# A scheduler's table of durations is replaced by measured ones, with a margin on what TensorE reads

## The chip, the cores and the metric

The kernel runs on one core of a Trainium2 chip. The metric is the device time of one launch, in microseconds (us). The core's engines each run their own queue of instructions in order: PE (TensorE, matmuls), DVE (VectorE), ACT (ScalarE), POOL (GpSimd) and SP (SyncE, which issues the DMAs here). An instruction waits at the head of its queue until its inputs are there, and everything behind it waits as well.

## The reference

Three layers in a row, on float32 data. The first is a linear attention with a complex decay per step; the second and third are wide layers on all 3072 tokens.

```python
def _attn_ref(q, k, v, a_re, a_im) -> np.ndarray:
    B, H, S, D = q.shape                       # 4, 8, 768, 48
    mag = np.sqrt(a_re * a_re + a_im * a_im)
    scale = np.minimum(mag, 0.999) / (mag + 1e-06)
    a_re_n, a_im_n = (a_re * scale, a_im * scale)
...
    for t in range(S):
        ar, ai = (a_re_n[:, :, t, :, None], a_im_n[:, :, t, :, None])
        new_re = ar * S_re - ai * S_im
        new_im = ar * S_im + ai * S_re
        kv = np.einsum('bhd,bhe->bhde', k[:, :, t], v[:, :, t])
        S_re, S_im = (new_re + kv, new_im)
        y[:, :, t] = np.einsum('bhd,bhde->bhe', q[:, :, t], S_re)
...
def _moe_ref(x, w_in, w_out) -> np.ndarray:    # 384 -> 2048 -> 384
    h = x @ w_in
    g = np.maximum(h, 0.0) + np.log1p(np.exp(-np.abs(h)))
    return (g @ w_out).astype(np.float32)
...
def _moe2_ref(x, w1, w2, w3, w_out) -> np.ndarray:   # 384 -> 1024 -> 1024 -> 384
    a = x @ w1
    b = x @ w2
    h = a * b @ w3
    return (h @ w_out).astype(np.float32)
```

## The kernel before

**Attention.** The 3072 tokens are 24 chunks of 128 (numbered `u`, six to a sequence). For a chunk, the decays `a` are loaded and normalised into `P` (ACT makes squares, logarithms and exponentials in `nt`; DVE the rest). DVE then runs a scan over pairs of chunks that multiplies the complex decays up: many multiplies into `tm` and additions back into `P`, on ever shorter and then longer strided slices. With the products of the decays DVE scales the queries and keys into `qkp`. PE transposes the keys (`ktp`), and the whole of `qkp` goes out to DRAM (`pd<-qkp`) and comes back in another layout with two gathers (`rs<-pd`). From `rs` PE computes the scores (`sc0`, `sc1`, four heads each), DVE masks them (`am`), and PE makes the chunk's output (`yp`) and the state's update (`stp`). ACT copies the output to `y`, six small DMAs (`y<-y`) move parts of it to other partitions, and it is cast into a block's input, `x` or `xh` with its remainder `xl`. The buffers `rs0` and `rs1` alternate between chunks.

**The wide layers.** Tokens are taken in blocks: block 0 is chunk 0, block 1 is chunks 1 and 2, and blocks 2 to 8 are three chunks (384 columns) each. In the second layer, each of 16 slices of the hidden width is a group of matmuls into `s1`, three ACT steps and a DVE step to `g`, a split of `g` into a rounded part `gh` and a remainder `gl`, and then matmuls that add into three sums `acc`. Blocks 0 and 1 use plain float32 (two records a matmul in the trace), the others three products of rounded parts. The weights arrive as raw float64 bits; DVE converts them (`w32`), interleaved with all this. The third layer runs behind block 8, with `w3` and `w_out` multiplied ahead into one matrix (`wpa`, `bwp`): groups `pa` and `pb`, their product `bg`, its split `bgh` and `bgl`, and again the sums `acc`. DVE meanwhile checks the raw weights (`ckr`) for their range.

**What sets the order.** The program records every instruction first (`Plan.add`), each with a cost on its engine and a latency until others may use its result, both from a fixed table in `cost`. `wait` gives the delay between a producer and a consumer. `together` makes one piece of a chunk's `yp` and `stp` matmuls. `flush` then runs a list scheduler (`run`): whenever an engine is free in the plan, it takes the most urgent instruction that is ready in the plan. It does so 16 times, each with priorities from the one before, and the plan that ends first is written out. The chip sees the resulting order of each queue and nothing of the planned times. DMAs are issued by SP in that order too.

So the table never costs time itself. Every record has the line of the recorded call (L185 before), so rows are told apart by the names of tiles.

Of the kernel before, what the change touches and what calls it, by code (L numbers as in the profile page):

```python
# [71 lines left out]
class Plan:  # L72
# [49 lines left out]
    def cost(self, eng, op, outs, ins):  # L122
        n = max(self.free_size(x) for x in (*outs, *ins))
        if eng == "SP":
            size = 4
            for _, n in outs[0].ap:
                size *= n
            cost = max(650 if n < 512 and self.on_chip(ins[0]) else 475, size / 360)
            return cost, 1100 + size / 360 + (950 if self.on_chip(outs[0]) else 2300) - cost
        if eng == "PE":  # L130
            n = self.free_size(outs[0])
            if op == "transpose":
                return 109, 200
            m = outs[0].ap[0][1]
            if ins[0].dtype == F32R:
                return max(n / 2.4 + 3, m / 1.2), 200
            return (0.73 * n + 38 if m <= 64 else max(n, m) / 0.6 + 5), 200
        if eng == "DVE":
            return 69 + n / (1.92 if op == "tensor_scalar" else 0.96), 200
        if eng == "ACT":  # L140
            return 120 + n / 1.4, 200
        return 160 + n * 2.08, 200

    def push(self, eng, call, pre, cost, lat):
        self.ops.append((eng, call, pre, cost, lat))
        return len(self.ops) - 1

    def add(self, engine, op, args, kw):
# [35 lines left out]
        def call():  # L184
            getattr(engine.unit, op)(*args, **kw)  # L185

        cost, lat = self.cost(engine.name, op, outs, ins)
        if self.group is None:
            me = self.push(engine.name, [call], pre, cost, lat)
# [17 lines left out]
    @contextmanager  # L207
    def together(self):

        self.group = self.push(None, [], set(), 57, 0)  # L210
        yield
        self.group = None

    def wait(self, p, s):
        eng, _, _, _, lat = self.ops[p]
        if eng == self.ops[s][0]:
            return {"DVE": 127, "PE": 0, "SP": lat}.get(eng, 200)
        return lat

    def run(self, before, after, ready, key, free):  # L220
# [1021 lines left out]
```

## Time and profile before

| | us |
|---|---|
| median of 3 runs | 995.36 |
| lowest and highest run | 994.29, 999.29 |
| the profiled execution's own time | 992.5 |
| its span, first to last instruction | 990.8 |
| PE busy | 885.4 |
| DVE busy | 786.6 |
| ACT busy | 530.6 |

The profiled execution is one run, taken with the hardware profiler; its rows give each instruction's start and duration, and a gap in front of an instruction is put down to what arrived last. Busy PE and DVE overlap almost wholly, so what counts is where PE stands idle, and whether DVE has room at that place.

### The profile page before, as it was taken

How to read it: one execution, taken by the hardware profiler on the slowest of the kernel's cores; microseconds unless marked ns; L12 is line 12 of the kernel's file. 1: busy time of each engine (PE TensorE's matmuls, PEld its weight loads, DVE VectorE, ACT ScalarE, POOL GpSimd, SP SyncE). 2: the span in 40 equal slices, each digit the busy share in tenths (PEclk: the TensorE clock that was granted, in tenths of full speed). 3: DMA queues.
4: the chain of work that ended last, by engine and by line, in shares of the span. 5: the costliest groups of instructions: out<-in, count | busy, mean ns of one | idle time of the engine just before them, and what ended most of it. 6: DMA issues, size and time to landing. Idle time of an engine off the chain costs nothing.

```text
span 990.8 us, 16846 instructions
## 1 busy us (share of the span) xinstructions
PE 885.4 (89%) x6169; PEld 859.6 (87%) x6169; DVE 786.6 (79%) x1773; ACT 530.6 (54%) x1132; POOL 5.4 (1%) x13
## 2 busy tenths in 40 slices
PE   0026999899999999999999989999999999999996
PEld 0026888798899999999999989999999999999996
DVE  6999999999999999999897587999888876322222
ACT  4246685677678686877876576564222222223222
POOL 2000000000000000000000000000000000000000
PEclk9999999999999999999999999999999999999998
DMA  8763744355454654455463465466888774010000
GB/s 307 243 188 80 174 117 121 109 119 120 118 156 115 157 127 122 115 111 162 118 147 105 104 170 166 137 174 201 240 263 265 223 240 157 1 48 25 1 25 27
DMA packets 84618, 138.67 MB, mean 140 GB/s; under 512 B 8112, under 2 KB 56880, under 8 KB 84528
## 3 DMA queue, kind: packets, MB, share of 16 engines
q1 hardware_dynamic: 84528, 137.53, 50.0%
q8 instruction: 50, 0.82, 0.4%
q14 instruction: 40, 0.33, 0.1%
HBM read 108.00 MB, written 28.31 MB: 138 GB/s over the span
## 4 chain that ended last, share of the span: by engine, by line
PE 48%; DVE 32%; DMA 12%; ACT 4%; issue 3%; SPq 0%; DVEq 0%; ACTq 0%
PE acc L185 17%; PE pa L185 8%; PE s L185 8%; PE pb L185 8%; DVE tm L185 7%; DVE P L185 7%; DMA rs<-pd 4%; PE wpa L185 3%; DVE qkp L185 2%; DVE g L185 2%; DVE w L185 2%; PE sc L185 2%; DMA a<-a_in 2%; DVE gl L185 2%; DMA ckr<-w3t 2%
## 5 line engine op out<-in xcount | busy, mean ns | idle before, releaser
L185 DVE TENSOR_TENSOR tm<-P 128x90 f32<-128x90 f32 (+3 forms) x240 | 145.4, 614 | 1.0
L185 ACT ACTIVATE e<-e 128x384 f32<-128x384 f32 (+2 forms) x288 | 136.5, 487 | 3.3
L185 DVE TENSOR_TENSOR bg<-pa,be 128x384 f32<-128x384 f32 x64 | 35.1, 554 | 90.4 <-PE pa L185 54.7
L185 ACT ACTIVATE e<-s 128x384 f32<-128x384 f32 (+2 forms) x144 | 64.4, 450 | 52.5 <-PE s L185 46.5
L185 DVE TENSOR_TENSOR P<-tm 128x45 f32<-128x45 f32 (+11 forms) x304 | 85.1, 341 | 1.2
L185 DVE SCALAR_TENSOR_TENSOR g<-s,e 128x384 f32<-128x384 f32 (+2 forms) x144 | 73.5, 513 | 11.6 <-ACT e L185 11.5
L185 PE MATMUL ktp<-ident,qkp 128*128 128x128 f32 x120 | 21.8, 288 | 67.3 <-DVE qkp L185 66.7
L185 ACT COPY be<-pb 128x384 f32<-128x384 f32 x64 | 30.4, 479 | 91.0 <-PE pb L185 88.7
L185 PEld LDWEIGHTS ktp<-ident,qkp 128*128 128x128 f32 x120 | 16.1, 149 | 69.4 <-issue 59.6
L185 ACT CAST bgh<-bg 128x384 fp32r<-128x384 f32 x64 | 32.7, 514 | 80.0 <-DVE bg L185 79.8
L185 PE MATMUL sc<-rs 112*128 112x128 f32 x384 | 58.3, 289 | 18.1 <-DMA rs<-pd 16.0
L185 PEld LDWEIGHTS sc<-rs 112*128 112x128 f32 x384 | 54.3, 202 | 21.0 <-issue 7.4
L185 DVE TENSOR_TENSOR gl<-g,gh 128x384 fp32r<-128x384 f32 x112 | 62.1, 557 | 10.0 <-ACT gh L185 9.7
L185 ACT CAST gh<-g 128x384 fp32r<-128x384 f32 x112 | 56.6, 508 | 20.9 <-DVE g L185 20.3
L185 DVE CUSTOM_DVE_ANT_0 ck<-ckr 128x384 f32<-128x384 f32 x80 | 43.4, 543 | 20.4 <-DMA ckr<-w3t 7.2
L185 DVE TENSOR_TENSOR bgl<-bg,bgh 128x384 fp32r<-128x384 f32 x64 | 35.1, 554 | 16.8 <-ACT bgh L185 16.3
L185 DVE TENSOR_REDUCE lims<-ck 128x1 f32<-128x384 f32 x80 | 43.0, 537 | 2.0
L185 PE MATMUL acc<-g,w 128*128 128x128 f32 (+1 forms) x192 | 39.9, 337 | 4.7 <-DVE g L185 4.7
L185 PE MATMUL wpa<-wo,w 128*128 128x384 f32 x192 | 41.8, 336 | 0.0
L185 ACT ACTIVATE nt<-a 128x768 f32<-128x768 f32 x24 | 20.3, 844 | 37.3 <-DMA a<-a_in 28.1
L185 PE MATMUL s<-x,w 128*128 128x128 f32 (+1 forms) x192 | 38.9, 338 | 1.2 <-ACT y L185 1.2
L185 DVE TENSOR_TENSOR am<-sc,mask 128x512 f32<-128x512 f32 x48 | 33.0, 688 | 8.4 <-PE sc L185 8.2
(323 smaller groups left out, 2569.7 us busy)
## 6 DMA issues: line engine op xcount, KB each, us to landing
pd<-qkp SPq DMA_DIRECT2D x24, 768.0 KB, 4.4
rs<-pd SPq DMA_DIRECT2D x48, 384.0 KB, 5.8
wr<-wio SPq DMA_DIRECT2D x32, 384.0 KB, 6.4
ckr<-wio SPq DMA_DIRECT2D x32, 384.0 KB, 3.6
a<-a_in SPq DMA_DIRECT2D x24, 384.0 KB, 3.4
qk<-qk_in SPq DMA_DIRECT2D x24, 384.0 KB, 3.3
w3r<-w3t SPq DMA_DIRECT2D x16, 384.0 KB, 3.9
w12r<-w SPq DMA_DIRECT2D x16, 384.0 KB, 3.6
```

The lines of the kernel that those rows point to most:

```text
L185: getattr(engine.unit, op)(*args, **kw)
```

## The change

The durations in `cost` are replaced. A DMA's latency no longer follows one formula: writes to DRAM count 5.2 us to landing, transfers inside the chip 2.3, loads from a DRAM tile of the kernel's own (that is `rs<-pd` and the reload of a block's `x`) 6.8, loads of inputs 2.5 plus size. Matmuls in rounded float32 go from n/2.4 + 3 to n/2.4 + 14 ns, short float32 ones get shorter, DVE operations with two widely strided inputs almost twice as long, ACT operations 105 + 0.88 n in place of 120 + n/1.4. A `together` group starts at 150 ns in place of 57. And `wait` adds 500 ns wherever PE is the consumer, 1500 if the producer is a DMA.

```diff
             cost = max(650 if n < 512 and self.on_chip(ins[0]) else 475, size / 360)
-            return cost, 1100 + size / 360 + (950 if self.on_chip(outs[0]) else 2300) - cost
+            if not self.on_chip(outs[0]):
+                land = 5200
+            elif self.on_chip(ins[0]):
+                land = 2300
+            elif hasattr(ins[0].tensor, "tag_meta"):
+                land = 6800
+            else:
+                land = 2500 + size / 360
+            return cost, max(land - cost, 0)
...
             if ins[0].dtype == F32R:
-                return max(n / 2.4 + 3, m / 1.2), 200
+                return n / 2.4 + 14, 250
...
         if eng == "DVE":
-            return 69 + n / (1.92 if op == "tensor_scalar" else 0.96), 200
+            far = [x for x in ins if x.ap[-1][0] >= 4 and x.ap[-1][1] > 1]
+            return 72 + n / (1.92 if op == "tensor_scalar" else 0.52 if len(far) > 1 else 0.95), 200
...
     def wait(self, p, s):
...
+        if self.ops[s][0] == "PE":
+            return lat + (1500 if eng == "SP" else 500)
         return lat
```

All queues keep the same instructions. Three places show how they move.

First, PE around the first scores of chunk 8 (`sc8_0`, which reads the gathered `rs0`), from the last transposes of the chunk's keys (`ktp8`). Before:

```order
L185 MATMUL ktp8_0_571<-ident_106,qkp8_529 128x128 x3
L185 MATMUL acc_472<-gh_2_9_551,ww8h_533 128x384
L185 MATMUL acc_470<-gl_2_8_539,ww8h_533 128x384
L185 MATMUL acc_470<-gh_2_9_551,ww8h_533 128x384
L185 MATMUL sc8_0_584<-rs0_121 128x128 x4
```

In the changed kernel, the last rows ahead of the same scores (47 matmuls of 384 columns now stand behind the last transpose):

```order
L194 MATMUL acc_472<-gl_2_10_561,ww10h_555 128x384
L194 MATMUL acc_471<-gl_2_10_561,ww10h_555 128x384
L194 MATMUL acc_470<-gh_2_11_569,ww10h_555 128x384
L194 MATMUL acc_470<-gh_2_11_569,ww11l_565 128x384
L194 MATMUL acc_471<-gh_2_11_569,ww10h_555 128x384
L194 MATMUL acc_471<-gh_2_11_569,ww11l_565 128x384
L194 MATMUL sc8_0_584<-rs0_121 128x128 x4
L194 MATMUL sc8_1_595<-rs0_121 128x128 x4
```

The scores moved behind the sums of slices 9, 10 and part of 11 of block 2, and both halves now stand together.

Second, PE between chunk 2's state update (`stp2`) and block 1, whose input is chunk 1's and chunk 2's output. Before, the rows that follow it:

```order
L185 MATMUL stp2_305<-v2_227,kT_123 48x48
L185 MATMUL s1_0_14_309<-x0_190,w32_14_293 128x128 x3
L185 MATMUL acc_216<-g_0_12_296,w32_12_278 128x128
L185 MATMUL acc_214<-g_0_12_296,w32_12_278 128x128
L185 MATMUL acc_216<-g_0_13_303,w32_13_287 128x128
L185 MATMUL acc_214<-g_0_13_303,w32_13_287 128x128
L185 MATMUL s1_0_15_312<-x0_190,w32_15_300 128x128 x3
L185 MATMUL acc_215<-g_0_12_296,w32_12_278 128x128
L185 MATMUL acc_215<-g_0_13_303,w32_13_287 128x128
L185 MATMUL sc3_0_333<-rs1_122 128x128 x3
```

In the changed kernel:

```order
L194 MATMUL stp2_305<-v2_227,kT_123 48x48
L194 MATMUL sc3_0_333<-rs1_122 128x128 x4
L194 MATMUL sc3_1_345<-rs1_122 128x128 x4
L194 MATMUL yp3_351<-rs1_122,S2_307 48x128 x2
L194 MATMUL yp3_351<-am3_0_334,v3_291 48x128 x2
```

The rest of block 0 now stands ahead of chunk 2's output. Between that and block 1 only chunk 3's scores, output and state update are left, with its `yp` directly behind its scores.

Third, DVE ahead of the second half of chunk 1's `qkp`, whose write lets its DMA start. Before:

```order
L185 TENSOR_SCALAR w32_9_255<-wr9_237 128x768
L185 TENSOR_TENSOR P1_141<-tm_165 128x96 x2
L185 TENSOR_SCALAR w32_10_262<-wr10_247 128x768
L185 TENSOR_TENSOR tm_166<-P1_141 128x192
L185 TENSOR_TENSOR n21_172<-n21_172,qk1_168 128x384
L185 TENSOR_TENSOR P1_141<-tm_166 128x48 x2
L185 SCALAR_TENSOR_TENSOR w32_9_255<-wr9_237,w32_9_255 128x768
L185 TENSOR_TENSOR tm_167<-P1_141 128x90
L185 TENSOR_TENSOR qkp1_179<-P0_133,n21_172 128x6x128
L185 TENSOR_TENSOR tm_167<-P1_141 128x90
L185 TENSOR_TENSOR qkp1_179<-P0_133,qk1_168 128x6x128
```

In the changed kernel:

```order
L194 SCALAR_TENSOR_TENSOR w32_9_255<-wr9_237,w32_9_255 128x768
L194 TENSOR_TENSOR tm_165<-P1_141 128x384
L194 TENSOR_TENSOR n21_172<-n21_172,qk1_168 128x384
L194 TENSOR_TENSOR P1_141<-tm_165 128x96 x2
L194 TENSOR_TENSOR qkp1_179<-P0_133,qk1_168 128x6x128
L194 TENSOR_TENSOR tm_166<-P1_141 128x192
L194 TENSOR_TENSOR qkp1_179<-P0_133,n21_172 128x6x128
L194 TENSOR_TENSOR P1_141<-tm_166 128x48 x2
L194 SCALAR_TENSOR_TENSOR w32_8_248<-wr8_229,w32_8_248 128x768
L194 TENSOR_TENSOR tm_167<-P1_141 128x90
```

Steps of the scan (`tm`, `P1`) and of the conversions (`w32_8`, `w32_10`) that stood ahead of `qkp1` stand behind it now.

## Rows read from the trace of the kernel before

**Rows 1.** The page: busy us, share and instructions; shares of the chain that ended last.

```profile
PE 885.4 (89%) x6169; PEld 859.6 (87%) x6169; DVE 786.6 (79%) x1773; ACT 530.6 (54%) x1132; POOL 5.4 (1%) x13
...
PE 48%; DVE 32%; DMA 12%; ACT 4%; issue 3%; SPq 0%; DVEq 0%; ACTq 0%
```

**Rows 2.** Busy time of each engine by stretch: from:to length, then busy (instructions).

```profile
core 0: us, PE busy (x) PEld busy (x) DVE busy (x) ACT busy (x) POOL busy (x), PEclk, DMA share, GB/s
0.00:59.70 59.70, 0.02 (x1) 0.05 (x1) 51.87 (x107) 18.64 (x32) 5.42 (x13) 1.00 0.74 258
59.70:87.70 28.00, 15.20 (x156) 13.72 (x156) 25.81 (x61) 13.61 (x24) 0.00 (x0) 0.94 0.66 155
87.70:257.20 169.50, 154.33 (x1215) 142.04 (x1214) 164.57 (x374) 119.60 (x285) 0.00 (x0) 0.99 0.49 123
257.20:393.30 136.10, 132.69 (x1044) 128.82 (x1043) 131.62 (x297) 102.38 (x220) 0.00 (x0) 1.00 0.52 130
393.30:594.30 201.00, 196.25 (x1545) 191.65 (x1544) 170.52 (x368) 143.89 (x309) 0.00 (x0) 1.00 0.52 130
594.30:983.90 389.60, 386.94 (x2217) 383.31 (x2215) 241.93 (x573) 132.44 (x267) 0.00 (x0) 1.00 0.46 139
```

**Rows 3.** PE's waits from 87.7 to 257.2: total us, times, longest.

```profile
PE sc L185 <- DMA rs<-pd: 4.9, 3, 2.2
PE acc L185 <- DVE g L185: 4.7, 5, 2.2
PE yp L185 <- DVE am L185: 1.3, 1, 1.3
PE s L185 <- ACT y L185: 1.2, 2, 0.8
PE sc L185 <- DVE am L185: 1.0, 1, 1.0
```

**Rows 4.** PE's waits from 257.2 to 594.3.

```profile
PE sc L185 <- DMA rs<-pd: 6.5, 3, 2.6
PE sc L185 <- DVE am L185: 1.1, 1, 1.1
PE acc L185 <- ACT gh L185: 0.3, 1, 0.3
```

**Rows 5.** DMA issues of the page, and the landings of `rs`, issued by SP.

```profile
rs<-pd SPq DMA_DIRECT2D x48, 384.0 KB, 5.8
...
DMA to landing us min/median/max: 4.3/5.8/7.8
```

**Rows 6.** PE's timeline at chunk 8: start, us, operation [idle before <-releaser].

```profile
238.47 1.13 PE L185 MATMUL sc<-rs 112*128 112x128 f32 x8 [2.19 <-DMA rs<-pd]
```

**Rows 7.** The chain that ended last: start, us, operation and count, near the end.

```profile
975.32 7.47 PE acc L185 x43
```

**Rows 8.** DVE groups by shape: count, busy us, mean ns of one, idle before.

```profile
L185 DVE TENSOR_TENSOR am<-sc,mask 128x512 f32<-128x512 f32 x48 | 33.0, 688 | 8.4 <-PE sc L185 8.2
...
L185 DVE TENSOR_TENSOR tm<-P 128x768 f32<-128x768 f32 x12 | 18.6, 1553 | 0.1
```

**Rows 9.** Timeline from chunk 5's output to block 2's first matmul.

```profile
176.88 0.39 PE L185 MATMUL yp<-am,v 128*48 128x128 f32 x4
...
178.03 1.17 ACT L185 COPY y<-yp 48x512 f32<-48x512 f32 x2
...
178.62 3.67 SPq L185 DMA_DIRECT2D y<-y  x6
...
185.38 0.87 PE L185 MATMUL s<-xh,ww0h 128*128 128x384 f32 x3
```

**Rows 10.** PE's timeline at chunk 1's scores.

```profile
80.77 3.59 PE L185 MATMUL sc<-rs 112*128 112x128 f32 x16 [3.96 <-DMA rs<-pd]
```

**Rows 11.** DVE's waits from 87.7 to 257.2.

```profile
DVE am L185 <- PE sc L185: 2.6, 3, 1.4
```

More of the change, by code (lines that the diff above doesn't have):

```diff
@@ L132, in cost @@
             if op == "transpose":
-                return 109, 200
+                return 109, 250
             m = outs[0].ap[0][1]
             if ins[0].dtype == F32R:
-                return max(n / 2.4 + 3, m / 1.2), 200
-            return (0.73 * n + 38 if m <= 64 else max(n, m) / 0.6 + 5), 200
+                return n / 2.4 + 14, 250
+            return (0.75 * n + 24 if m <= 64 else max(n, m) / 0.6 + 5), 250
         if eng == "DVE":
-            return 69 + n / (1.92 if op == "tensor_scalar" else 0.96), 200
+            far = [x for x in ins if x.ap[-1][0] >= 4 and x.ap[-1][1] > 1]
+            return 72 + n / (1.92 if op == "tensor_scalar" else 0.52 if len(far) > 1 else 0.95), 200
         if eng == "ACT":
-            return 120 + n / 1.4, 200
+            return 105 + 0.88 * n, 200
         return 160 + n * 2.08, 200
@@ L208, in together @@
     def together(self):
-        self.group = self.push(None, [], set(), 57, 0)
+        self.group = self.push(None, [], set(), 150, 0)
         yield
```

## The prediction

> **What bounds the kernel now.** I read the busy table of the page first [rows 1]: TensorE is busy 885.4 us of a span of 990.8, VectorE 786.6. Both averages hide stages, so next come the stretches, cut where a block's first matmul runs: 87.7 us is the first matmul of block 0, 257.2 that of block 3, 393.3 that of block 5, 594.3 that of block 8 [rows 2]. Up to 59.7 us TensorE has nothing and VectorE works alone. From 87.7 to 257.2 TensorE is busy 154.33 of 169.5 us and VectorE 164.57: VectorE has 4.9 us of idle time there, so it is the closer bound. From 257.2 to 393.3 it is 132.69 and 131.62 of 136.1. From 393.3 to 594.3 TensorE leads, 196.25 against 170.52 of 201.0, and from 594.3 to 983.9 it runs at 386.94 of 389.6 with VectorE half idle. So what can still be won is TensorE's idle time: 15.2 us from 87.7 to 257.2, 3.4 to 393.3, 4.8 to 594.3, 2.7 to 983.9, and the first of these only as far as VectorE allows.
>
> Then the waits: who held TensorE up. From 87.7 to 257.2 the five largest make 13.1 us: scores waiting for the gathered rows `rs` 4.9, output sums waiting for `g` 4.7, and 3.5 for others [rows 3]. From 257.2 to 594.3 they are 6.5 for `rs`, 1.1 for `am`, 0.3 for `gh` [rows 4]. The reader is to see that 11.4 of these are six waits of up to 2.6 us for one kind of DMA: TensorE stands in order, so everything behind a score waits with it.
>
> **The change, part by part.** No instruction is added or removed; only places in the queues change, so every term is a wait that goes or comes.
>
> *DMA landings.* The old table lets `rs` land 3.1 us after its issue (1100 + 1092 + 950 ns), the new one 6.8, and 1.5 more before TensorE may use it. The trace has a median of 5.8 us, and 4.3 to 7.8 between the ends [rows 5]. So the old plan put scores about 3 us ahead of their data, and the new one puts them a little behind. Chunk 8 shows it: three 384-column matmuls stood between its last transpose and its first score, and TensorE waited 2.19 us [rows 6]; now 47 stand there. At 173.7 ns each (43 in 7.47 us, [rows 7]) the 44 more are 7.7 us. The other five waits are covered too, by my count of the rows: chunk 4 gets 23 matmuls where none stood, chunk 7 gets 73 for 1, chunk 9 some 13.6 us of block 3 for 2.4, chunk 17 gets 19 matmuls more (3.3 us), chunk 23 gets 15 more (2.6 us, as long as its wait, the longest; and its `qkp` has fewer VectorE rows ahead).
>
> Here a page of the Trainium skill speaks against the change. "DMA: Bandwidth & Descriptors", section "Anatomy of one DMA — SWDGE (gpsimd) path", fits about 2.0 us plus bytes over 436 GB/s; for 393,216 bytes that is an estimate of 2.9 us, and by it the old 3.1 was right and all six waits would have another cause. The trace's shortest landing is 4.3 us, on a hardware queue and from a scattered read, so the measurement decides.
>
> *Engine durations.* The old table gives a 384-column matmul 163 ns, the new one 174; the trace 173.7. It gives a strided 768-element multiply on VectorE 869 ns, the new one 1549; the trace 1553 with the tail that overlaps the next instruction, and 12 of them stand in the scans [rows 8]. Its old plan thus let both engines drift late against their partners by different amounts.
>
> "TensorE: Matmul & The Clock Gate" in the Trainium skill, section "Back-to-back issue gap", has N/2.4 + 2.5 ns for matmuls by themselves, an estimate of 162.5 ns for 384 columns. By that the old figure was the right one; the 173.7 of this trace decides for the new one.
>
> *The margin.* Every input of TensorE now counts as 500 ns after its producer's latency. In order, TensorE runs what stands first, so a margin costs nothing while other rows fill it. Counted over the rows, the work between a block's `s1` group and the first sum that reads its `g` grows in every block (smallest gap in block 0 from 2.3 to 3.7 us). That covers the 4.7 us of waits for `g`.
>
> *What comes in its place.* A TensorE that waits less runs out of rows sooner. A block can't begin before the last chunk's output has been copied, shifted by six small DMAs and cast. In chunk 5 that took from 177.3 us (176.88 + 0.39) to 185.4: 8.1 us with little to spare [rows 9]. In the old order the work between that output and the next block was more than this, or about it: 10.2, 7.5 and 9.8 us ahead of blocks 1, 2 and 3, counted in rows. In the new one it is some 6, 5.5 and 7. The rows show it for block 1: sums and `s1` groups of block 0 stood between, now only chunk 3's own work. I expect new waits of about 2, 2.5 and 1 us, 5.5 together, and 1.5 at chunk 3, where the `yp` group stands right behind its scores and has to wait for both `am`, 0.69 us each.
>
> *The head.* The scores of chunk 1 waited 3.96 us for `rs` [rows 10]. Of VectorE's rows ahead of `qkp1`, a step each of `w32_8` and `w32_10` and three short steps of the scan have gone behind it, some 2 us by my count, while chunk 0's `am` moves back by as much. I take 1 us, between 0 and 2.
>
> **The sum**, against the profiled execution's own 992.5 us:
> - head: −1 (0 to −2).
> - 87.7 to 257.2: 13.1 us of listed waits go, 5.5 + 1.5 come, which leaves 6; VectorE gives at most its 4.9 us of idle time, of which 2.6 are waits for scores [rows 11]. I take −4, most of it (0 to −9.8, which is TensorE's 15.2 less the 5.5).
> - 257.2 to 594.3: idle 8.2, of which 7.9 listed; one new wait of 1 at block 5. I take −6 (0 to −8.2).
> - 594.3 to the end: −0.5 of 2.7. The order of the check rows alters little there.
>
> Together −11.5: 981.0. The median of the runs shown lies 2.9 us above the profiled execution and the lowest run 1.8, so I add 2: **983**.
>
> **The rivals.**
> - *More is won.* VectorE turns out not to be the limit, because its idle time and its late starts both shrink with the better durations: all the lower bounds, −2 −9.8 −8.2 −2.7 = −22.7, give 972. For it: TensorE's margins grow nearly everywhere in the new order. Against: VectorE at 97% from 87.7 to 257.2. Chance 0.17, taking in what lies below 978.
> - *The waits only move.* The waits for `rs` and `g` reappear as waits at the block starts and for `am`. If VectorE sets the pace up to 393.3, the first part and the 3.4 us after it are worth nothing, and of the 4.8 after that some 2 stay: 992.5 + 2 − 1 − 2 = about 992. For it: VectorE has 32% of the chain that ended last [rows 1], though TensorE alone sets the pace behind 594.3. Chance 0.18.
> - *Slower: scores too late for VectorE.* VectorE runs in order too, and its `am` stands where it stood, while chunk 8's scores move back by 7.7 us of TensorE's rows. If TensorE hasn't won that much by then, VectorE stands at `am` with the scan queued behind it, in the stretch in which it has only 4.9 us to give. With nothing won the 7.7 come on top: 992.5 + 2 + 7.7 − 2 = about 1000. It decides once TensorE's gain ahead of chunk 8 is below some 4 us. The page on DMAs would make this the likely case, its landings being too short for such a late place; the 4.3 to 7.8 us in the trace make it the unlikely one. Chance 0.10.
>
> **Chances and range.** My forecast, 978 to 990, has 0.55. About 0.5%, 5 us, is what a measurement of this kernel can tell from no change. So faster than 990.4: 0.55 + 0.17 = 0.72; within: 0.18; slower: 0.10. The range of 8 in 10 goes from 971 (just under the case in which all is won) to 996 (half-way from the moved waits to the slower case).
>
> **What would show it.** Waits of scores for `rs` behind 100 us: from 11.4 us to under 3. Waits of sums for `g`: under 2. TensorE's waits for `y` or `xh` at block starts: a new row of 3 to 7 us. The first matmul of block 3 at about 252 in place of 257.2, that of block 8 at about 583 in place of 594.3, and the time behind block 8 unchanged within 2 us. VectorE's waits for scores shouldn't exceed 8 us from 87 to 257. I'm wrong if block 3 begins later than 257, or if the gain is lost again between 393 and 594, where VectorE has room.

## The result, and the profile after

The changed kernel takes 980.34 us in the median of 4 runs (979.71 to 981.5), the kernel before 994.83 (994.19 to 999.29, 4 runs). The ratio is 0.9847, with a 95% interval of 0.982 to 0.9874: faster by 1.5%. The forecast was 983, with 971 to 996. The profiled execution of the changed kernel is one of 979.78 us; its span is 978.0, 12.8 less than before.

The stretches come first again, now cut where the same matmuls run: block 0's first at 88.0 us, block 3's at 250.6, block 5's at 385.1, block 8's at 582.3 (columns as in [rows 2]). The last cut alone is not the same one: 983.9 in [rows 2] lies behind the closing matmul `okt`, 970.0 here lies ahead of it.

```profile
core 0: us, PE busy (x) PEld busy (x) DVE busy (x) ACT busy (x) POOL busy (x), PEclk, DMA share, GB/s
0.00:57.50 57.50, 0.00 (x0) 0.01 (x1) 51.06 (x106) 18.39 (x32) 5.42 (x13) 1.00 0.75 265
57.50:88.00 30.50, 17.00 (x157) 15.27 (x157) 29.18 (x68) 15.27 (x27) 0.00 (x0) 0.89 0.63 148
88.00:250.60 162.60, 153.39 (x1227) 141.97 (x1227) 160.95 (x367) 118.27 (x284) 0.00 (x0) 1.00 0.49 121
250.60:385.10 134.50, 133.28 (x1055) 129.98 (x1055) 130.14 (x294) 104.70 (x224) 0.00 (x0) 1.00 0.57 144
385.10:582.30 197.20, 195.94 (x1533) 191.29 (x1534) 174.20 (x375) 140.82 (x304) 0.00 (x0) 1.00 0.51 131
582.30:970.00 387.70, 383.63 (x2201) 380.75 (x2199) 241.09 (x566) 131.66 (x265) 0.00 (x0) 1.00 0.45 138
```

Against [rows 2]: block 0 starts 0.3 us later, the stretch from block 0 to block 3 is 6.9 us shorter (169.5 to 162.6), and that from block 3 to block 8 is 5.4 shorter (337.1 to 331.7). From block 8 to the end of the last sum (982.78 us before, 969.87 now) it is 0.9 shorter (388.5 to 387.6), and what follows is as long as before (8.0 and 8.1). From block 3 to block 8 PE now stands idle 2.5 us (331.7 − 133.28 − 195.94), where it was 8.2. DVE's idle time from block 0 to block 3 fell from 4.9 to 1.7 us (162.60 − 160.95). DVE also has 3.6 us less to do there (164.57 to 160.95). For 2.6 of it, six more of its instructions now run ahead of block 0: 80.24 us of work (51.06 + 29.18) in place of 77.68 (51.87 + 25.81). The other 1.1 moved behind the beginning of block 3.

PE's waits from block 0 to block 3 (88.0 to 250.6 us) answer to [rows 3]: total us, times, longest.

```profile
PE s L194 <- ACT xh L194: 3.5, 2, 1.9
PE s L194 <- ACT x L194: 2.2, 2, 1.5
PE ktp L194 <- DVE g L194: 1.5, 3, 0.8
PE yp L194 <- DVE am L194: 1.2, 1, 1.2
PE s L194 <- DVE g L194: 0.6, 1, 0.6
PE sc L194 <- DMA rs<-pd: 0.4, 1, 0.4
```

Those from there to block 8 (582.3 us) answer to [rows 4]:

```profile
PE s L194 <- ACT xh L194: 2.5, 2, 1.6
PE sc L194 <- DVE g L194: 0.8, 1, 0.8
PE sc L194 <- DVE am L194: 0.4, 1, 0.4
PE stp L194 <- DVE g L194: 0.2, 1, 0.2
```

The wait of 1.6 us for `xh` is that of block 3's first matmul; it stands at the cut and is in both lists. The scores' 11.4 us for the gathered rows have become 0.4, and the sums' 4.7 for `g` are gone from the list. In their place stand `s` groups that wait for `x` and `xh`: PE has used up its block and waits for the next one's input. The transfers themselves are no faster. Their landings in the changed kernel:

```profile
DMA to landing us min/median/max: 4.3/6.1/8.1
```

In the head, PE's timeline shows why nothing came of the 1 us. The first line is from the kernel before, the rest from the changed one:

```profile
74.84 1.08 PE L185 MATMUL yp<-am,v 128*48 128x128 f32 x16 [0.83 <-ACT nt L185]
...
68.39 3.75 PE L194 MATMUL sc<-rs 112*128 112x128 f32 x16 [0.95 <-DMA rs<-pd]
75.31 1.89 PE L194 MATMUL yp<-am,v 128*48 128x128 f32 x16 [3.17 <-issue]
76.92 1.89 PE L194 MATMUL stp<-v,kT 128*64 128x48 f32 x32
78.87 1.13 PE L194 MATMUL sc<-rs 112*128 112x128 f32 x8
81.73 1.64 PE L194 MATMUL sc<-rs 112*128 112x128 f32 x8 [1.73 <-ACT y L194]
...
88.00 3.65 PE L194 MATMUL s<-x,w 128*128 128x128 f32 x30 [0.69 <-ACT x L194]
```

The scores of chunk 1 no longer wait for the gathered rows (3.96 us in [rows 10]), but chunk 0's `yp` now waits 3.17 us, and the second half of chunk 1's scores 1.73. The first is put down to no producer by the profile, but DVE's second `am` of chunk 0 ends at 75.21 us, 0.1 us ahead of `yp`. It ended at 74.73 before, although chunk 0's scores now begin 1.9 us sooner (68.39 against 70.31).

The clock takes part in this as well. Busy time by stretch, the first line again from the kernel before:

```profile
80.70:84.40 3.70, 3.63 (x18) 3.54 (x20) 1.80 (x5) 0.84 (x1) 0.00 (x0) 0.55 0.25 81
...
75.30:78.90 3.60, 3.53 (x49) 3.40 (x49) 3.60 (x9) 1.56 (x2) 0.00 (x0) 0.53 0.95 169
81.70:86.20 4.50, 4.47 (x40) 4.21 (x42) 4.50 (x9) 4.03 (x8) 0.00 (x0) 0.62 0.07 15
```

A granted clock of 0.53 is 1.2 GHz, the lower of its two levels, for nearly the whole stretch. Before, one such stretch followed the wait of 3.96 us; now one follows the wait of 3.17 and one that of 1.73. The 16 matmuls of `yp` took 1.89 us where they took 1.08. In sum PE starts 2.2 us sooner (57.5 against 59.7), is busy 1.8 us longer in the head (15.20 to 17.00, mean clock 0.94 to 0.89) and idle 0.7 longer (12.80 to 13.50), which makes the 0.3.

### The profile page after: what moved, and what is told of

Its sections match the earlier page's. It is cut to its first block, busy times and chain, and to the rows that moved or that the text cites. A ratio compares the mean times of both kernels' runs of the same rounds, so it can differ in the third digit from the quotient of the medians.

```text
span 978.0 us, 16869 instructions
## 1 busy us (share of the span) xinstructions
PE 883.5 (90%) x6169; PEld 859.3 (88%) x6169; DVE 787.4 (81%) x1773; ACT 529.5 (54%) x1132; POOL 5.4 (1%) x13
## 4 chain that ended last, share of the span: by engine, by line
PE 64%; DVE 10%; DMA 7%; issue 2%; ACT 1%; SPq 0%; DVEq 0%; ACTq 0%
PE acc L194 23%; PE s L194 14%; PE pa L194 8%; PE pb L194 8%; PE sc L194 3%; PE yp L194 3%; PE wpa L194 3%; DMA a<-a_in 2%; DVE tm L194 2%; DMA ckr<-wio 2%; DVE P L194 2%; DMA ckr<-w 1%; PE stp L194 1%; DVE ck L194 1%; DVE g L194 1%
## 5 line engine op out<-in xcount | busy, mean ns | idle before, releaser
L194 PEld LDWEIGHTS ktp<-ident,qkp 128*128 128x128 f32 x120 | 15.6, 148 | 68.6 <-issue 57.5
L194 PE MATMUL sc<-rs 112*128 112x128 f32 x384 | 53.0, 285 | 4.3 <-ACT y L194 1.7
L194 PEld LDWEIGHTS sc<-rs 112*128 112x128 f32 x384 | 50.3, 198 | 6.2 <-ACT y L194 1.9
L194 PE MATMUL yp<-am,v 128*48 128x128 f32 x384 | 36.9, 282 | 4.4 <-issue 3.2
L194 ACT COPY xob<-acc 128x384 f32<-128x384 f32 x24 | 11.4, 481 | 52.5 <-PE acc L194 37.4
L194 PE MATMUL wpa<-wo,w 128*128 128x384 f32 x192 | 39.1, 334 | 0.0
L194 PE MATMUL s<-x,w 128*128 128x128 f32 (+1 forms) x192 | 36.0, 330 | 3.1 <-ACT x L194 2.2
```

## The experiments

The change has three parts: the landings of the DMAs, the durations of the engines, and the margin in `wait`. Each kernel below computes everything. Times are medians with the ratio to runs of the kernel before on the same chip, and its 95% interval. The waits named are those of scores for the gathered rows from 100 to 600 us, unless another stretch is given; the kernel before has 11.4 us of them in six waits.

**Each part alone, and the two without the margin.** The edits take the change's own lines, one part at a time:

```diff
 # d_only: the landings alone
+            if not self.on_chip(outs[0]):
+                land = 5200
...
 # e_only: the costs of PE, DVE and ACT, and of a group, alone
+                return n / 2.4 + 14, 250
...
 # m_only: the margin alone
+        if self.ops[s][0] == "PE":
+            return lat + (1500 if eng == "SP" else 500)
 # de: the changed kernel without the margin
```

> The kernel before with the new DMA landings alone. My theory (each part of the table removes its own waits): the scores' waits for the gathered rows fall from 11.4 us behind 100 us to under 3, sums still wait 3 to 5 us for g, and the time is some 6 us shorter, about 988 to 990. If the margin does it all: no change, 995. If any other order is simply as good as any other and the one before was an unlucky one: a time anywhere from 980 to 1000 that doesn't follow the waits for the gathered rows.

Measured: 984.84 us, ratio 0.9892 (0.987 to 0.9914). No wait for the gathered rows is left; sums wait 2.1 us for `g` from 100 to 250 us, less than the 3 to 5 I had expected. The landings alone give some 70% of the gain (1.1 of 1.5%), more than I had expected.

> The kernel before with the new durations of PE, DVE and ACT alone. My theory: the waits for the gathered rows stay near 11 us, since the landings are as before; the drift of PE and DVE against each other shrinks, so waits of sums for g fall below 3 us; about 990. If the landings do it all: 995. If the order is luck: anything from 980 to 1000.

Measured: 1035.11 us, ratio 1.0389 (1.0361 to 1.0417). This is far outside what any of the theories gave: the measured durations by themselves cost 38 us (1035.11 against 997.06 before on the same chip), the "40 us" of what follows. PE's waits from 100 to 600 us begin with

```profile
PE sc L186 <- DMA rs<-pd: 27.4, 12, 4.3
PE ktp L186 <- DVE qkp L186: 1.6, 1, 1.6
```

and DVE, whose `am` stands in its queue for the scores, waits from 60 to 700 us (8.2 us in the kernel before):

```profile
DVE am L186 <- PE sc L186: 32.9, 25, 4.1
```

So my theory, that each part removes its own waits, falls. Sums wait only 0.5 us for `g` from 100 to 250 us, but twelve waits for the gathered rows came, and both engines stood still in them. The granted clock fell too. Busy time in five stretches of 20 us of this kernel:

```profile
220.00:240.00 20.00, 17.34 (x115) 16.85 (x115) 15.70 (x28) 12.26 (x26) 0.00 (x0) 0.91 0.30 85
240.00:260.00 20.00, 16.64 (x138) 15.55 (x134) 17.52 (x34) 12.32 (x28) 0.00 (x0) 0.91 0.42 92
...
340.00:360.00 20.00, 15.69 (x90) 15.37 (x89) 15.21 (x28) 13.48 (x30) 0.00 (x0) 0.91 0.70 169
360.00:380.00 20.00, 17.87 (x144) 17.20 (x143) 16.63 (x49) 11.25 (x24) 0.00 (x0) 1.00 0.49 112
380.00:400.00 20.00, 20.00 (x167) 19.67 (x166) 20.00 (x39) 17.36 (x36) 0.00 (x0) 1.00 0.44 119
```

A mean of 0.91 is a part of the stretch at 1.2 GHz and the rest at 2.4; it stands where PE had idle time, though not in every such stretch. Over the span PE is busy 904.9 us with the same 6169 matmul records that took 885.4 before [rows 1]. These 19.5 us are somewhat under half of the 44.8 by which the profiled span is longer (1035.6 against 990.8). The lower clock is my reading of them, and its size fits: the mean granted clock of the span is 0.974 against 0.994, so 26.9 us of full clock were not granted (0.026 × 1035.6) against 5.9, 21 us more. Of the other 25.3 us, all idle time, 20.7 are waits for the gathered rows: over the whole span they rose from 16.0 to 36.7.

> The kernel before with the margin alone: 500 ns on what PE reads, 1500 on what it reads from a DMA. My theory: 3.1 + 1.5 us still falls short of a median landing of 5.8, so 4 to 8 us of waits for the gathered rows stay; waits for g and am nearly go; about 988 to 990. If the margin does it all: 980. If the measured durations do it all: 995.

Measured: 990.25 us, ratio 0.994 (0.9915 to 0.9965); 4.5 us of waits for the gathered rows in five waits. The time and these waits came as expected. What I had wrong is `g`: its waits did not nearly go. Sums still wait 2.3 us for it in one wait (3.4 before), and `sc`, `s` and `ktp` groups 6.1 us more.

> The changed kernel without the margin: landings and engine durations as measured. My theory: waits for the gathered rows under 4 us (6.8 covers most landings, 1.5 of margin is missing), waits for g of 2 to 4 us, about 983 to 986. If the margin does it all: 995. If the margin only delays PE: faster than with it, 976.

Measured: 985.85 us, ratio 0.9897 (0.9875 to 0.9919); no wait for the gathered rows, and one block starts with a wait of 5.1 us for `xh`. Within the expectation; beside the landings alone the durations add nothing that these intervals can tell.

**Which number the 40 us hang on.** A new theory: in an exact plan of PE no slack is left by accident, so a false landing costs in full. The first kernel below adds to the engine durations only the 6.8 us for loads from the kernel's own DRAM tiles; the second changes one number of the kernel before.

```diff
 # e_rs: e_only, and
-            return cost, 1100 + size / 360 + (950 if self.on_chip(outs[0]) else 2300) - cost
+            land = 6800 - cost if not self.on_chip(ins[0]) and hasattr(ins[0].tensor, "tag_meta") else 0
+            return cost, max(land, 1100 + size / 360 + (950 if self.on_chip(outs[0]) else 2300) - cost)
 # b_pe174: the kernel before, and
-                return max(n / 2.4 + 3, m / 1.2), 200
+                return n / 2.4 + 14, 200
```

> The engine durations, and of the landings only the 6.8 us for loads from the kernel's own DRAM tiles (the gathered rows and a block's reload). Theory A: the 1035 us with the engine durations alone come from the gathered rows' old 3.1 us, which an exact plan of PE no longer covers by accident; then this one number takes back nearly all of it, 984 to 990, with under 4 us of waits for the gathered rows and a granted clock above 0.99. Theory B: the engine durations themselves give a bad order (DVE's strided cost or ACT's put rows in the wrong places); then it stays above 1010.

Measured: 987.69 us, ratio 0.9904 (0.9879 to 0.9928), granted clock 0.995. From 100 to 600 us no wait for the gathered rows is left; PE's largest group of waits there is

```profile
PE s L187 <- ACT xh L187: 2.9, 1, 2.9
```

One number takes back 47 us from 1035.11. Theory A holds and B falls, for the set of durations as a whole.

> The kernel before with one number changed: a matmul in rounded float32 costs n/2.4 + 14 ns, not n/2.4 + 3. Theory A: the old 163 ns let the real PE run late against its plan, which hid DMA landings; with 174 the waits for the gathered rows rise above 18 us and the time to 1005 to 1030. Theory B: one correct number does no harm, 990 to 997.

Measured: 1021.18 us, ratio 1.0233 (1.0203 to 1.0262). The time is where theory A put it, but its reason is only partly there. PE's largest groups of waits from 100 to 600 us:

```profile
PE sc L185 <- DMA rs<-pd: 12.1, 7, 2.8
PE acc L185 <- ACT gh L185: 5.8, 6, 1.7
PE s L185 <- ACT xh L185: 4.2, 4, 2.4
PE acc L185 <- DVE g L185: 2.3, 4, 0.9
```

Those for the gathered rows rose only from 11.4 to 12.1 us, not above 18. What rose is the others: for `gh` from 0.8 (0.3 of it in [rows 4]) to 5.8, for `xh` from nothing to 4.2. Behind 600 us another 7.2 in eight waits are for `bgh` (0.2 before), and 4.0 in the head are for `x`. Over the whole span PE waits 23.3 us for ACT's `x`, `xh`, `gh` and `bgh`, where it was 1.0. The profiled span is 28.8 us longer (1019.6): 17.2 of it idle time, 11.6 busy time (897.0), at a mean granted clock of 0.988. It seems that the short price of a matmul had hidden ACT's steps: the old table prices one of 384 columns at 394 ns, the new one at 443, and with all engine durations replaced these waits for ACT are only 4.0 us. No run changed ACT's price by itself, so this stays a reading. That one true number alone does harm is shown for this seed; no second one was run for it.

**Is it the draw?** The scheduler has one noisy round, so another seed gives another order with the same table.

```diff
-SEED = 214
+SEED = 1
```

> The kernel before with another seed of the scheduler's one noisy round. If the table decides: within 1% of before, 987 to 1003, with 8 to 20 us of waits for the gathered rows. If the order of before is an unlucky or a lucky draw: more than 1% off.

Measured: 997.62 us, ratio 1.0014 (0.9997 to 1.003); 14.5 us of waits for the gathered rows in eleven. Against this one other seed, the kernel before was no unlucky draw.

> The changed kernel with the same other seed. If the table decides: 975 to 988, again with under 4 us of waits for the gathered rows. If its gain is a draw: 990 or more.

Measured: 987.87 us, ratio 0.99 (0.9871 to 0.9928); no wait for the gathered rows from 100 to 600 us, one of 4.9 in the head. Still 1% faster than before, but 0.5% slower than with seed 214.

> The engine durations alone with seed 1. Theory A: again far slower than before, 1015 to 1045, with over 15 us of waits for the gathered rows. If the 1035 us were a bad draw of the scheduler: 1005 or less.

Measured: 1018.19 us, ratio 1.0239 (1.0202 to 1.0277); 19.6 us of waits in eleven. The engine durations alone are slow with this seed too, by 22 us (996.01 before on this chip) in place of 38. With this table the two seeds are 17 us apart.

> The changed kernel without the margin, with seed 1, beside 985.9 with seed 214 and 987.9 for the margin with seed 1. If the margin is worth something beyond the draw: 990 to 996. If it is only a draw: 980 to 989.

Measured: 987.88 us, ratio 0.9927 (0.9901 to 0.9953), beside 987.87 with the margin and the same seed. With seed 1 the margin is worth nothing. And beside the engine durations alone with the same seed, the true landings take back 30 us (1018.19 to 987.88).

**The margin without the landings, and a shorter landing.** The first kernel is the changed one with the old line for DMAs, the second has one number changed:

```diff
 # em: the old landings
+            return cost, 1100 + size / 360 + (950 if self.on_chip(outs[0]) else 2300) - cost
 # a_rs29
-                land = 6800
+                land = 2900
```

> The changed kernel with the old DMA landings: engine durations and margin, so the gathered rows count as 3.1 + 1.5 us. Theory A (an exact PE plan needs slack ahead of every PE input, and either a true landing or a margin gives it): the margin takes back most of the 40 us of the engine durations alone, 988 to 1000; waits for the gathered rows 4 to 12 us, since 4.6 us is still short of most landings. Theory C (only the true landing of the gathered rows matters): it stays above 1015.

Measured: 992.98 us, ratio 0.9965 (0.9948 to 0.9983), with 4.4 us of waits for the gathered rows in four. The margin takes back 42 us from 1035.11, so theory C falls: slack ahead of every input does nearly what the true landing does.

> The changed kernel with 2.9 us in place of 6.8 for loads from the kernel's own DRAM tiles, the estimate from the Trainium skill's page on DMA; the margin of 1.5 us stays. My theory: 4.4 us is below the median landing of 5.8, so 5 to 10 us of waits for the gathered rows come back, and the time is 985 to 995. If the landing of the gathered rows doesn't matter beside the margin: 978 to 983.

Measured: 1001.8 us, ratio 1.0068 (1.0047 to 1.009): slower than before, and worse than I had expected. 13.1 us of waits for the gathered rows in ten are back, as the head of PE's waits from 100 to 600 us shows:

```profile
PE sc L194 <- DMA rs<-pd: 13.1, 10, 3.2
PE ktp L194 <- DVE qkp L194: 3.2, 1, 3.2
```

Here 2.9 + 1.5 us, that is 4.4, is in force for the scores, against 3.1 + 1.5 in the kernel above. With this one landing false and everything else as in the changed kernel, the time is 21 us longer. The 0.2 us between 4.4 and 4.6 can hardly make the 9 us between these two kernels; they also differ in the other landings, and neither has a second seed. So the waits that came back are shown, but how much of the 21 us is a draw is not.

## Why the prediction was right, and what it had wrong

**The sum.** I gave −11.5 us on the profiled execution; the span is 12.8 shorter. By terms:

- Head: −1 forecast, +0.3 measured. Chunk 1's wait went as forecast, but I let `am` of chunk 0 move back "by as much" and didn't price it: `yp` waits 3.17 us for it. I also left out the clock, which makes PE's work in the head 1.8 us longer. The start, 2.2 us sooner, is lost again.
- Block 0 to block 3: −4 forecast, −6.9 measured. I had limited it to most of DVE's 4.9 us of idle time. That bound was wrong, since it held DVE's work in the stretch for fixed. DVE's idle time fell by 3.3 us and its work there by 3.6, which together are the 6.9. Of the work, 2.6 us moved ahead into the head and 1.1 behind the beginning of block 3 (540 instructions up to there before, 538 now). So the head, in which PE won nothing, is where DVE won room. The term was mis-sized, its direction right.
- Block 3 to block 8: −6 forecast, −5.4 measured.
- Behind block 8: −0.5 forecast, −0.9 measured up to the last sum and +0.1 behind it.
- The 2 us from the profiled execution to the median were 0.6 (979.78 to 980.34).

The terms erred both ways, so the total is closer than the two terms ahead of block 3 deserve. The sum was read off this one order; the same table with seed 1 gives 988, so which seed was set moves the time by more than my total was off. Two figures in my working are 0.1 off, with no effect on the forecast: 15.2 less 5.5 is 9.7, and 44 matmuls of 173.7 ns are 7.6 us. Of the signs that I named, all came: the waits for the gathered rows, the sums' for `g`, the new row at block starts, block 3 at 250.6 and block 8 at 582.3, and no wait of DVE for scores from block 0 to block 3.

**DMA landings.** The six waits are gone, as counted from the rows. That the landings are the cause is shown from both sides: alone they give 0.9892, and with one of them put back to a short value (2.9 us) the changed kernel is slower than the one before. Beside the engine durations, the 6.8 us alone take back 47 us, and all the true landings take back 30 with the other seed. All six kernels with 6.8 us for the gathered rows (changed, `d_only`, `de`, `e_rs`, and the two with seed 1) lie between 980 and 988 us and have at most 0.4 us of waits for them behind 100 us; all eight without it, the kernel before and its second seed among them, lie between 990 and 1035. The waits for the gathered rows are not all that sets the time, though: the kernel with the one true matmul price has 12.1 us of them, hardly more than the kernel before, and takes 1021.

**The two rules weighed.** In the Trainium skill, the page "DMA: Bandwidth & Descriptors" (section "Anatomy of one DMA — SWDGE (gpsimd) path") gave an estimate of 2.9 us; the measured landings of 4.3 to 8.1 and the kernel planned with 2.9 speak against using it for this transfer. The page "TensorE: Matmul & The Clock Gate" of the Trainium skill (section "Back-to-back issue gap") gave an estimate of 162.5 ns for a matmul by itself; the trace's 173.7 is the rate at which they run, but the experiments add something I hadn't seen: the plan with the shorter, false figure was the better one as long as the rest of the table was false.

**Engine durations.** This step failed. I wrote that the old plan "let both engines drift late against their partners by different amounts", as if exact durations could only help, and gave them no term of their own. Alone they cost 38 us, or 22 with the other seed. My reading is that the drift had been useful: a PE that runs later than planned finds its inputs there. In the changed kernel this does no harm because the landings are true as well; beside them the durations are worth nothing that can be told (0.9892 without them, 0.9897 with them).

**The margin.** This step was wrong too. I gave it the 4.7 us for `g`. In the changed kernel those waits of sums are gone, but the margin alone leaves 2.3 us of them, and the changed kernel without it has only 1.5 and lies at 0.9897; with seed 1 there is no difference. It acts as a substitute for what the table has wrong: with the false landings it recovers 42 us, with the true ones nothing that a second seed confirms. The 0.5% by which seed 214 with the margin beats the other kernels with true landings is a draw as far as these runs can tell.

**New waits at block starts.** Forecast 2, 2.5 and 1 us at blocks 1 to 3 and 1.5 at chunk 3's `yp`; the waits after are 3.5 for `xh` (two waits, blocks 2 and 3), 1.5 for `x` at block 1 (the other 0.7 of its row stand ahead of block 0), and 1.2 for `am`. That is 6.2 in all against 7, so the step held. At block 5 the wait forecast as 1 is 0.9.

**The rivals.** "The waits only move" happened in part and was in the sum. "Scores too late for VectorE" didn't: no wait of DVE for scores is left from block 0 to block 3, where it was 2.6 us [rows 11]. Its opposite is what the engine durations alone show, where scores stand too early for their data and DVE waits 32.9 us for them. "More is won" didn't come.

## What to carry to other kernels

In a table that orders work, correct the entry with the largest absolute error first, here a landing of 3.1 us that takes about 6: correcting the small ones alone can take away slack that hid it. Where landings can't be measured, a margin on every input of the busiest engine is a partial substitute: here it recovered 42 of the 47 us beside exact engine durations, but beside the old table it gave 0.6% where the true landings gave 1.1. Before a gain of half a per cent is put down to a table, run a second seed: here two seeds of one table were up to 1.5% apart (1.0389 and 1.0239 with the engine durations alone).

## What the runs showed of the hardware that was not expected

The gathered rows (384 KB from DRAM, read in another order than they were written) land in 4.3 to 8.1 us, median 6.1, in the changed kernel, and no order made that shorter: the medians of all 14 kernels lie between 5.7 and 6.2. And short PE waits seem to cost more than their own length. In the kernel with the engine durations alone the same matmuls are busy 904.9 us in place of 885.4, with stretches of 20 us at a mean granted clock of 0.91 where PE stood idle 2.7 to 4.3 us of them. In the head of the changed kernel 16 matmuls behind a wait of 3.17 us took 1.89 us at a granted clock of 0.53, and 1.08 at full clock in the kernel before. That the wait lowers the clock is read from what follows what; no run set it by itself.
